# The first step of seven block products moves into the second plain block, and output rows get six buffers

## The chip, the cores and the metric

The kernel runs on one core of a Trainium2 chip. The metric is the device time of one execution in microseconds (us). The runs of the kernel before took 783.31 to 784.70 us, median 784.04. A core has a matrix engine (TensorE, PE in the profile), a vector engine (VectorE, DVE), a scalar engine (ScalarE, ACT), GpSimd (POOL) and SyncE (SP), which issues most transfers. Each engine works through its own list of instructions in the order of the program; semaphores tie the lists together.

## The reference, cut to what matters

```python
# 1. attention without softmax, RMS norm        -> x [2304, 512]
# 2. eight experts, each token goes to one       -> x [2304, 512]
# 3. the dense layer pair, d_model 512, d_ff 2048:
h = x @ w_in                                              # [2304, 2048]
g = np.maximum(h, 0.0) + np.log1p(np.exp(-np.abs(h)))     # softplus
return g @ w_out                                          # [2304, 512]
```

All inputs are float32. The change touches part 3 alone, the last 380 us of the kernel.

## The kernel before, in words

**Precision.** Every float32 operand of a matmul is held as a high part (a cast on ACT) and a low part (value minus high part, on DVE). A product is then three matmuls: high by high, high by low, low by high.

**Tokens.** Part 3 takes the 2304 tokens as two *plain blocks* of 384 and two *passes* of 768 (`NPAS`).

**Plain blocks** (`mlp_step`, L1039). For each of the 16 slices f of 128 hidden units: 12 matmuls of 384 columns (`mlp1`, L951) fill a PSUM bank `tp_t`; softplus follows in three pieces, each one step later than the one before (`soft_a`, `soft_b`, `soft_c`, L971 to L998); then 9 matmuls of 512 columns (`mlp2`, L1017) add the slice into three output banks `acc_t`. So in step f the PE does `mlp1` of f and `mlp2` of f-2, while ACT and DVE do the cast of f-2, the logarithm of f-1 and the absolute value and exponential of f. `side(s)` (L1594) puts work for the passes behind each step: sums and differences of the input blocks (`x_sum`, L1108), their splits (`x_split`, L1101) and those of the weights (`w_sums`, L1120).

**Passes.** Here the first matrix product is taken in 2 by 2 blocks with seven block products instead of eight (the scheme of Strassen and Winograd). A pass has eight *steps* s of 256 hidden units, so there are 16 steps, s = 0 to 15. `prod(s, n)` (L1140) is product n: 6 matmuls of 384 columns into one of two PSUM accumulators, `strip["a"]` and `strip["b"]`, in the order 1, 2, 6, 5, 7, 3, 4. Between products the accumulators are read out: `keep_a(0..2)` and `c12` are copies on ACT (L1165, L1174), `c11`, `c22` and `c21` additions on DVE (L1168, L1171, L1177). A product that starts or goes on in an accumulator has to wait for the read-out before it. The results are two halves of 768 columns, *a* (c11 and c22) and *b* (c21 and c12).

Each half goes through softplus one step later: `pa` is absolute value and exponential on ACT (L1185, L1186) and adding 1 on DVE (L1187); `pa2` a correction on DVE (L1191) and the logarithm on ACT (L1192); `pb` a maximum-and-add and a subtraction on DVE (L1196, L1197); `pc` the cast on ACT (L1203) and the low part on DVE (L1204). `pc` also queues six *units*; a unit (L1213) is three matmuls of 512 columns into one of six output banks. `strip_step` (L1230) writes the order out by hand: products, units and these pieces.

For the first eight steps `w_raw(s+1)` loads raw weights (L1118), `w_sums` makes four sums (L1127), casts them (L1129), takes the low part (L1131) and stores both for the second pass (L1133); `w_load` (L1115) brings the plain weights, `w2_load` (L1138) those of the second layer. All of these stand in SP's list in program order.

**The end of the blocks** (L1630 to L1663). Step 0 has a form of its own: its products 1 and 2 stand between the last two `mlp_step` calls, the other five and half *a* of its softplus behind them.

**Output rows.** `store_rows` (L1006) copies an output bank to a row buffer and sends it off with an indirect transfer of POOL. Odd rows alternate between two buffers `orow`, even rows all use one place in the tile `ma`.

Of the kernel before, what the change touches and what calls it, by code (L numbers as in the profile page):

```python
# [25 lines left out]
def attention_moe_mlp(tc, q, k, v, g_norm, emb, tau, w1, w2, w_in, w_out, out, caps=CAPS):  # L26
# [20 lines left out]
    NBLK = 2  # L47
    blocks = [(i * HB, HB) for i in range(NBLK)]
# [1020 lines left out]
    def plan():  # L1069
# [4 lines left out]
            [xw[:, 1024 * i:1024 * i + 1024] for i in range(4)],  # L1074
# [5 lines left out]
        strip["g"] = [(mr[:, 0:2 * HB], mr[:, 2 * HB:4 * HB]), tuple(t_[:, 0:2 * HB] for t_ in wm[0, 7])]  # L1080
        strip["s"] = [ma[:, 2432 + HB * i:2432 + HB * (i + 1)] for i in range(3)]
# [7 lines left out]
    def x_src(ps, nm, c):  # L1089
# [50 lines left out]
    def prod(s, n):  # L1140

        a, b = strip["a"], strip["b"]
        wop, xop, dst, start = {
            1: ("A11", "B11", a, True), 2: ("A12", "B21", b, True), 6: ("S2", "T2", a, False), 5: ("S1", "T1", a, False),
            7: ("S3", "T3", b, True), 3: ("S4", "B22", a, False), 4: ("A22", "T4", b, False),
        }[n]
        for c in range(2):
            if wop[0] == "A":
                at = (2 * (int(wop[2]) - 1) + c) * 256 + 128 * (int(wop[1]) - 1)
                w = strip["w"][s % 2][0:2]  # L1150
            else:
# [42 lines left out]
    def pb(kind, s):  # L1194
        h, e, u = soft[kind, s]
        nc.vector.scalar_tensor_tensor(out=u, in0=h, scalar=0.0, in1=u, op0=ALU.max, op1=ALU.add)  # L1196
        nc.vector.tensor_tensor(out=u, in0=u, in1=e, op=ALU.subtract)  # L1197

    def pc(kind, s):
        h, e, u = soft[kind, s]  # L1200
        gh, gl = strip["g"][strip["m"] % 2]
        strip["m"] += 1
        nc.scalar.copy(gh, u)  # L1203
        nc.vector.tensor_tensor(out=gl, in0=u, in1=gh.bitcast(F32), op=ALU.subtract)  # L1204
        for i in range(2):
# [24 lines left out]
    def strip_step(s, extra):  # L1230

        todo = [x for x in extra]

        def more(n=1):
# [38 lines left out]
        if s:  # L1273
            pb("b", s - 1)
        more(2)
        c12(s)
        unit(1)
# [313 lines left out]
    pools["ma"] = ma_pool.tile([128, 3584], F32, name="ma")  # L1591
    pools["mr"] = ma_pool.tile([128, 1536], F32R, name="mr")

    def side(s):  # L1594

        if s in (3, 14):
            for p in range(4 * (s // 14), 4 * (s // 14) + 4):
                for i in range(2):
                    nc.sync.dma_start(out=ws[p, i], in_=wm[0, p][i].bitcast(F32))
                    if p % 4 > 1:  # L1600
                        nc.sync.dma_start(out=ws2[p // 4 * 2 + p % 2, i], in_=wm[1, p][i].bitcast(F32))
        f = s - NF
        if f == 2:
            plan()
            strip["raw"] = dp.tile([128, 1024], F32, name="raws", tag="raw64", bufs=2)
            w_raw(0)
        if f == 4:
            sums = dp.tile([128, 1024], F32, name="sums", tag="raw64", bufs=2)
            strip["gen"] = w_sums(0, sums.rearrange("p (j n) -> p j n", j=4))
        if f in (4, 5, 6):  # L1610
            next(strip["gen"])
            next(strip["gen"])
        if f == 9:
            strip["raw"] = dp.tile([128, 1024], F32, name="raws", tag="raw64", bufs=2)
            w_raw(1)
        for nm, split in {
            7: (("B11", 1),), 8: (("T1", 0),), 9: (("B21", 1),), 10: (("T1", 1), ("T2", 0)),
            11: (("T2", 1), ("T3", 0)), 12: (("T4", 0), ("T3", 1)), 13: (("B22", 1),), 14: (("T4", 1),),
        }.get(f, ()):
            for c in range(2):  # L1620
                (x_split if split else x_sum)(0, nm, c)

# [7 lines left out]
    strip["e"] = dp.tile([128, 1024], F32, name="ce", tag="raw64", bufs=2)[:, 0:2 * HB]  # L1630
    strip["a"], strip["b"] = (acc_tile()[:, 0:HB] for _ in range(2))
    x_sums = x2[:, :, 2 * HB:2 * HB + 256]
    w_load(1, (0, 1))
    gen_ = w_sums(1, x_sums)
    prod(0, 1)
    keep_a(0)
    mlp_step(last)
    prod(0, 2)
    mlp_step(last + 1)
    w2_load(2)  # L1640
    w2_load(3)
    while rest:
        store_rows(*rest.pop(0))
    prod(0, 6)
    c11(0)
    keep_a(1)
    prod(0, 5)
    keep_a(2)
    for _ in range(3):
        next(gen_)  # L1650
    prod(0, 7)
    c22(0)
    pa("a", 0)
    pa2("a", 0)
    prod(0, 3)
    c12(0)
    pb("a", 0)
    for _ in range(3):
        next(gen_)
    prod(0, 4)  # L1660
    c21(0)
# [154 lines left out]
```

## Time and profile before

| | us |
|---|---|
| median of the three runs | 784.04 |
| the profiled execution | 786.2 |
| its span, first to last instruction | 784.2 |
| PE busy (92% of the span) | 720.3 |
| DVE busy (72%) | 565.2 |
| ACT busy (56%) | 438.9 |

The profiled execution is 2.0 us longer than its span. Busy time is a union over overlapping instructions, so a PE that runs at the lower of its two clock levels (the profile gives the granted clock as a share of 2.4 GHz, 0.5 being 1.2 GHz) is busy and slow at once. The interesting figure of a stretch is its length against the matmul columns in it. In the profiled execution the second plain block ends near 472 us; step 1 begins at 476.61, step 2 at 501.74, step 3 at 521.02, step 7 at 589.65, step 9 at 627.42, step 11 at 670.19, step 15 at 737.00 us.

### The profile page before, as it was taken

The numbers are of one execution on the slowest core, as the hardware profiler recorded it, in microseconds if no ns is written. First come the engines' busy times: TensorE is split into PE (matmuls) and PEld (weight loads), VectorE is DVE, ScalarE is ACT, GpSimd is POOL, SyncE is SP. The second block draws the span as 40 slices with busy tenths as digits, with TensorE's granted clock in tenths as the row PEclk, the third lists the DMA queues.
The fourth block names the chain that finished last, engine by engine and source line by source line (L and its number), as shares of the span: only waits on it lengthen the run. The fifth ranks groups of instructions, "written<-read, shape, count | busy, mean of one in ns | idle before, by whom it ended". The sixth has DMA issues, their size and how long they took to land.

```text
span 784.2 us, 11874 instructions
## 1 busy us (share of the span) xinstructions
PE 720.3 (92%) x4267; PEld 638.7 (81%) x4267; DVE 565.2 (72%) x990; ACT 438.9 (56%) x783; POOL 265.6 (34%) x203
## 2 busy tenths in 40 slices
PE   8885899999999999999999996899998969999983
PEld 5884599999999999989899885788886858888862
DVE  5589888887887888779767873576777835666661
ACT  2686585575676666567565643455555654454452
POOL 5365168867777876737210001000000030000002
PEclk9997899999999999999999997799999979999998
DMA  9994699988889998563912036433552264245102
GB/s 241 274 291 165 212 299 318 306 265 272 296 272 314 295 310 286 196 232 124 374 41 81 1 108 207 155 134 135 211 218 108 108 241 162 107 134 221 76 0 83
DMA packets 82754, 154.36 MB, mean 197 GB/s; under 512 B 14708, under 2 KB 43404, under 8 KB 82690
## 3 DMA queue, kind: packets, MB, share of 16 engines
q1 hardware_dynamic: 79170, 143.70, 55.7%
q0 software_dynamic: 3344, 9.80, 3.3%
q8 instruction: 35, 0.57, 0.3%
q14 instruction: 29, 0.24, 0.1%
q10 hardware_dynamic: 176, 0.05, 0.0%
HBM read 114.71 MB, written 38.81 MB: 196 GB/s over the span
## 4 chain that ended last, share of the span: by engine, by line
PE 55%; issue 19%; DVE 14%; ACT 7%; DMA 3%; POOL 1%; SPq 1%; ACTq 0%; DVEq 0%; POOLq 0%
PE acc_t L895 9%; PE acc_t L897 8%; PE acc_t L896 8%; PE acc_t L1028 3%; PE acc_t L1027 3%; PE acc_t L1026 3%; PE tp_t L897 3%; PE tp_t L895 3%; PE tp_t L896 3%; PE acc_t L1226 2%; PE tp_t L1332 1%; PE acc_t L1224 1%; PE acc_t L1225 1%; DVE ma L1196 1%; DVE ma L1197 1%
## 5 line engine op out<-in xcount | busy, mean ns | idle before, releaser
L903 POOL TENSOR_TENSOR wl<-st,wh 128x1024 fp32r<-128x1024 f32 x64 | 156.1, 2443 | 57.4 <-ACT wh L901 56.5
L1015 POOL DMA_INDIRECT out_dram<-ma,idx x9 | 8.9, 986 | 317.0 <-ACT ma L1014 315.2
L901 ACT CAST wh<-st 128x1024 fp32r<-128x1024 f32 x72 | 74.7, 1045 | 37.9 <-PE acc_t L896 17.2
L895 PE MATMUL acc_t<-hh,wh 128*128 128x368 f32 (+7 forms) x256 | 81.1, 317 | 0.0
L895 PE MATMUL acc_t<-xh,wh 128*128 128x368 f32 (+7 forms) x256 | 78.5, 307 | 1.1 <-ACT x L1555 0.7
L897 PE MATMUL acc_t<-hh,wl 128*128 128x368 f32 (+7 forms) x256 | 78.1, 305 | 0.9 <-DVE wl L903 0.9
L896 PE MATMUL acc_t<-xl,wh 128*128 128x368 f32 (+7 forms) x256 | 78.2, 305 | 0.0
L896 PE MATMUL acc_t<-hl,wh 128*128 128x368 f32 (+7 forms) x256 | 78.0, 305 | 0.0
L897 PE MATMUL acc_t<-xh,wl 128*128 128x368 f32 (+7 forms) x256 | 78.0, 305 | 0.0
L1192 ACT ACTIVATE ma<-ma 128x768 f32<-128x768 f32 x32 | 27.1, 846 | 63.8 <-DVE ce L1191 63.8
L895 PEld LDWEIGHTS acc_t<-xh,wh 128*128 128x128 f32 x256 | 48.2, 188 | 2.1 <-ACT x L1555 1.4
L1196 DVE SCALAR_TENSOR_TENSOR ma<-x,ma 128x768 f32<-128x768 f32 x32 | 30.7, 958 | 26.3 <-ACT ma L1192 26.3
L895 PEld LDWEIGHTS acc_t<-hh,wh 128*128 128x128 f32 x256 | 48.1, 188 | 1.4 <-DVE hl L1538 0.3
L897 PEld LDWEIGHTS acc_t<-hh,wl 128*128 128x128 f32 x256 | 48.2, 188 | 1.2 <-DVE wl L903 1.2
L896 PEld LDWEIGHTS acc_t<-xl,wh 128*128 128x128 f32 x256 | 48.2, 188 | 0.6 <-DVE xl L1361 0.6
L897 PEld LDWEIGHTS acc_t<-xh,wl 128*128 128x128 f32 x256 | 48.2, 188 | 0.0
L896 PEld LDWEIGHTS acc_t<-hl,wh 128*128 128x128 f32 x256 | 48.2, 188 | 0.0
L1533 ACT ACTIVATE hh<-acc_t 128x368 fp32r<-128x368 f32 (+7 forms) x64 | 27.7, 433 | 23.1 <-PE acc_t L897 22.6
L1187 DVE TENSOR_SCALAR ma<-ce 128x768 f32<-128x768 f32 x32 | 17.9, 559 | 30.9 <-ACT ce L1186 30.8
L1165 ACT COPY ma<-tp_t 128x384 f32<-128x384 f32 x45 | 21.4, 476 | 27.0 <-PE tp_t L1159 26.8
L978 ACT ACTIVATE ma<-tp_t 128x384 f32<-128x384 f32 x30 | 14.8, 492 | 36.0 <-PE tp_t L897 36.0
L1538 DVE SCALAR_TENSOR_TENSOR hl<-acc_t,hh 128x368 fp32r<-128x368 f32 (+7 forms) x64 | 29.9, 474 | 6.6 <-ACT hh L1533 6.4
(410 smaller groups left out, 2201.1 us busy)
## 6 DMA issues: line engine op xcount, KB each, us to landing
st<-in_moe_w_dram SPq DMA_DIRECT2D x64, 512.0 KB
xs<-ws SPq DMA_DIRECT2D x24, 512.0 KB
raw<-in_moe_w_in_dram SPq DMA_DIRECT2D x16, 512.0 KB
raw<-in_moe_w_out_dram SPq DMA_DIRECT2D x16, 512.0 KB
wd<-pre_p SPq DMA_DIRECT2D x32, 256.0 KB
wh<-ws SPq DMA_DIRECT2D x11, 512.0 KB
wl<-ws SPq DMA_DIRECT2D x11, 512.0 KB
ws<-wh SPq DMA_DIRECT2D x10, 512.0 KB
```

Source lines behind the costliest of these rows:

```text
L895: nc.tensor.matmul(ps_, wh, xh, start=start, stop=False)
L896: nc.tensor.matmul(ps_, wh, xl, start=False, stop=False)
L897: nc.tensor.matmul(ps_, wl, xh, start=False, stop=stop)
L901: nc.scalar.copy(h, raw)
L903: eng.tensor_tensor(out=l, in0=raw, in1=h.bitcast(F32), op=ALU.subtract)
L1026: nc.tensor.matmul(mt[b][t_], gh[:, cs_], wh[:, f % 2, :], start=f == 0, stop=False)
L1027: nc.tensor.matmul(mt[b][t_], gh[:, cs_], wl[:, f % 2, :], start=False, stop=False)
L1028: nc.tensor.matmul(mt[b][t_], gl[:, cs_], wh[:, f % 2, :], start=False, stop=f == NF - 1)
L1192: nc.scalar.activation(out=u, in_=u, func=AF.Ln)
L1196: nc.vector.scalar_tensor_tensor(out=u, in0=h, scalar=0.0, in1=u, op0=ALU.max, op1=ALU.add)
L1533: nc.scalar.activation(out=hh[:, m, :C], in_=p[:, :C], func=AF.Relu)
L1538: nc.vector.scalar_tensor_tensor(out=hl[:, m, :C], in0=p[:, :C], scalar=0.0, in1=hh[:, m, :C].bitcast(F32), op0=ALU.max, op1=ALU.subtract)
```

## The change

Three things are done, and buffers are laid out anew to make room for them.

1. **Step 0 stands inside the second plain block.** `side` is given an own table: behind plain step f = 9 come product 1 and `keep_a(0)`, behind 10 product 2, behind 11 product 6, behind 12 product 5, behind 13 product 7 and `c22`, behind 14 product 3, `c12` and the beginning of softplus of half a. Product 4 stands ahead of the call that ends slice 14, the rest of softplus of half a between the calls for slices 14 and 15. Input sums and weight sums start earlier, and weight sums of steps 0 and 1 both end within the block.
2. **Six row buffers for the passes.** Rows 0 and 1 use the two `orow` buffers, rows 2 to 5 free columns of the four parts of `x2`.
3. **Another order in `strip_step`.** The absolute value of half a stands in front of `keep_a(0)`, that of half b in front of `keep_a(2)`; `pc` of half a comes in front of product 5; both DVE pieces of `pb` for b stand together; the four weight sums come in one piece after `keep_a(0)`; step 15 starts softplus of its half a itself. `w_sums` now works in place, in the tile that the raw weights are loaded into.

```diff
     def store_rows(b, t_):
...
-        o = dp.tile([128, DM], F32, name="orow", tag="dec_a", bufs=2) if i % 2 else pools["ma"][:, 5 * HB:5 * HB + DM]
+        if b >= NBLK and t_ > 1:
+            o = x2[:, t_ - 2, 2 * HB:2 * HB + DM]
+        elif i % 2 or b >= NBLK:
+            o = dp.tile([128, DM], F32, name="orow", tag="dec_a", bufs=2)
+        else:
+            o = pools["ma"][:, 5 * BLK:5 * BLK + DM]
...
+    def w_sums(s, raw):
+        a = raw.rearrange("p (k n) -> p k n", k=4)
+        a11, a12, a21, a22 = (a[:, 2 * j:2 * j + 2, 128 * i:128 * i + 128] for i in range(2) for j in range(2))
+        h, l = strip["w"][s % 2][2:4]
+        for o, p, m, op in ((a22, a21, a22, ALU.add), (a21, a11, a21, ALU.subtract), (a11, a22, a11, ALU.subtract), (a12, a12, a11, ALU.subtract)):
+            nc.vector.tensor_tensor(out=o, in0=p, in1=m, op=op)
+            yield
+        nc.scalar.copy(h, raw)
...
     def strip_step(s, extra):
...
         prod(s, 1)
         if ("b", s - 2) in soft:
             pc("b", s - 2)
-        more()
+        if ahead:
+            pa("a", s - 1)
         keep_a(0)
+        more(4)
+        if ahead:
+            pa1("a", s - 1)
+        more(1)
         unit(2)
         prod(s, 2)
-        more(2)
-        if s > 1:
-            pa("a", s - 1)
+        if ahead:
+            pa2("a", s - 1)
         unit(1)
         prod(s, 6)
-        if s > 1:
-            pa2("a", s - 1)
         c11(s)
+        if ahead:
+            pb("a", s - 1)
         keep_a(1)
-        if s > 1:
-            pb("a", s - 1)
-        more()
+        if ahead:
+            pb2("a", s - 1)
+            pc("a", s - 1)
+        more(1)
         unit(3)
         prod(s, 5)
-        if s > 1:
-            pc("a", s - 1)
+        pa("b", s - 1)
         keep_a(2)
         more(2)
         unit(2)
         prod(s, 7)
-        if s:
-            pa("b", s - 1)
+        pa1("b", s - 1)
         c22(s)
-        if s:
-            pa2("b", s - 1)
+        pa2("b", s - 1)
+        if final:
+            pa("a", s)
         unit(2)
         prod(s, 3)
...
+    def side(s):
...
+        if f == 9:
+            strip["a"], strip["b"] = (acc_tile()[:, 0:HB] for _ in range(2))
+            prod(0, 1)
+            keep_a(0)
...
+        if f == 14:
+            strip["e"] = [raw_tile()[:, 0:2 * HB]]
+            prod(0, 3)
+            c12(0)
+            pa("a", 0, x2[:, 1, 0:2 * HB])
+            pa1("a", 0)
...
     w_load(1, (0, 1))
+    next(strip["sums", 1])
+    prod(0, 4)
+    c21(0)
+    pa2("a", 0)
     mlp_step(last)
+    pb("a", 0)
+    pb2("a", 0)
+    pc("a", 0)
     mlp_step(last + 1)
```

ACT's list at the end of the second plain block, before: L978 and L979 are absolute value and exponential of slice 15, L1165 is `keep_a(0)` of step 0, L996 the casts of slices 14 and 15, L986 the logarithm of slice 15, L1014 the row copies, L1185 the absolute value of step 0's half a.

```order
L978 ACTIVATE ma<-tp_t 128x384
L979 ACTIVATE ma<-ma 128x384
L1165 COPY ma<-acc_t 128x384
L996 CAST mr<-ma 128x384
L986 ACTIVATE ma<-ma 128x384
L996 CAST mr<-ma 128x384
L1014 COPY orow<-acc_t 128x512
L1014 COPY ma<-acc_t 128x512
L1014 COPY orow<-acc_t 128x512
L1165 COPY ma<-acc_t 128x384 x2
L1185 ACTIVATE ce<-x_1100 128x768
```

The same place after the change: L1186, L1190, L1196 and L1212 are absolute value, exponential, logarithm and cast of step 0's half a, the three casts of L996 those of slices 13, 14 and 15.

```order
L1186 ACTIVATE raws<-x_1100 128x768
L1190 ACTIVATE raws<-raws 128x768
L996 CAST mr<-ma 128x384
L986 ACTIVATE ma<-ma 128x384
L978 ACTIVATE ma<-tp_t 128x384
L979 ACTIVATE ma<-ma 128x384
L1196 ACTIVATE x_1100<-x_1100 128x768
L996 CAST mr<-ma 128x384
L986 ACTIVATE ma<-ma 128x384
L1212 CAST wh_b_4772<-x_1100 128x768
L996 CAST mr<-ma 128x384
L1019 COPY orow<-acc_t 128x512
```

Each of the three casts that `mlp2` of slices 13 to 15 needs now has an instruction of step 0's half a in front of it.

ACT's list over one step of the first pass, before: L1203 is the cast of a half, L1165 `keep_a`, L1185, L1186 and L1192 absolute value, exponential and logarithm, L1129 the cast of the weight sums, L1174 `c12`.

```order
L1203 CAST wh_b_4772<-ma 128x768
L1165 COPY ma<-tp_t 128x384
L1185 ACTIVATE ce<-x_1100 128x768
L1186 ACTIVATE ce<-ce 128x768
L1192 ACTIVATE ma<-ma 128x768
L1165 COPY ma<-tp_t 128x384
L1203 CAST mr<-ma 128x768
L1165 COPY ma<-tp_t 128x384
L1129 CAST wh_4154<-x_1100 128x1024
L1185 ACTIVATE ce<-x_1100 128x768
L1186 ACTIVATE ce<-ce 128x768
L1192 ACTIVATE ma<-ma 128x768
```

After, from the same cast on: L1212 is the cast, L1186, L1190 and L1196 the three functions, L1164 `keep_a`, L1133 the cast of the weight sums, L1173 `c12`.

```order
L1212 CAST mr<-ma 128x768
L1186 ACTIVATE raws<-x_1100 128x768
L1164 COPY ma<-tp_t 128x384
L1190 ACTIVATE raws<-raws 128x768
L1133 CAST wh_4154<-raws 128x1024
L1196 ACTIVATE ma<-ma 128x768
L1164 COPY ma<-tp_t 128x384
L1212 CAST wh_b_4772<-ma 128x768
L1186 ACTIVATE raws<-x_1100 128x768
L1164 COPY ma<-tp_t 128x384
L1190 ACTIVATE raws<-raws 128x768
L1196 ACTIVATE ma<-ma 128x768
```

The absolute values passed a `keep_a` each, and the cast of the weight sums went from the second half of the step to the first.

On POOL the order of the rows' transfers is the same; the six rows of a pass now leave from six different places, where they alternated between two.

## Rows read from the trace of the kernel before

**Rows 1.** Windows by stage: length, each engine's busy time (count), PEclk, DMA share, GB/s
```profile
456.61:476.61 20.00, 18.45 (x91) 16.03 (x91) 9.13 (x19) 9.37 (x19) 2.92 (x3) 1.00 0.56 183
476.61:501.74 25.13, 15.61 (x62) 12.89 (x61) 11.82 (x18) 8.63 (x13) 0.00 (x0) 0.80 0.47 173
501.74:521.02 19.28, 19.09 (x78) 16.38 (x79) 13.47 (x20) 9.18 (x13) 0.00 (x0) 0.82 0.40 143
521.02:589.65 68.63, 65.22 (x313) 55.97 (x312) 52.38 (x77) 36.79 (x52) 0.00 (x0) 1.00 0.48 176
589.65:627.42 37.77, 33.37 (x157) 27.81 (x156) 29.16 (x45) 22.26 (x38) 0.00 (x0) 1.00 0.30 112
627.42:670.19 42.77, 36.30 (x158) 30.20 (x156) 21.05 (x28) 20.06 (x31) 7.08 (x6) 0.88 0.51 185
670.19:737.00 66.81, 65.44 (x313) 55.74 (x312) 40.74 (x53) 33.39 (x49) 0.00 (x0) 1.00 0.43 158
737.00:784.20 47.20, 31.85 (x133) 24.41 (x131) 20.42 (x26) 18.44 (x27) 5.83 (x6) 0.90 0.10 35
680.95:686.89 5.94, 5.94 (x32) 5.40 (x30) 4.31 (x6) 1.72 (x4) 0.00 (x0) 1.00 0.01 3
```

**Rows 2.** Timeline of PE, two matmuls behind long waits: start, duration, [wait and releaser]
```profile
483.81 0.80 PE L1224 MATMUL acc_t<-wh,mr 128*128 128x512 f32 x1 [6.00 <-ACT mr L1203]
...
761.21 0.80 PE L1224 MATMUL acc_t<-wh_b,mr 128*128 128x512 f32 x1 [2.08 <-ACT mr L1203]
```

**Rows 3.** Chain that ended last, end of step 2: start, share of the chain, what
```profile
514.27 1.05 ACT xs L1129
515.32 0.75 ACT ce L1185
...
516.10 0.86 ACT ce L1186
...
516.98 0.56 DVE ma L1187
517.54 0.47 DVE x L1171
518.00 0.88 DVE ce L1191
...
518.90 0.86 ACT ma L1192
...
519.78 0.97 DVE ma L1196
...
520.77 0.97 DVE ma L1197
...
521.76 0.84 ACT wh_b L1203
...
522.63 0.97 DVE wl_b L1204
```

**Rows 4.** Timeline of all engines behind the load of raw weights for step 2
```profile
484.69 0.46 SPq L1118 DMA_DIRECT2D raws<-wd  x1
...
490.05 0.42 DVE L1127 TENSOR_TENSOR x<-raws 128x256 f32<-128x256 f32 x1 [4.43 <-DMA raws<-wd]
```

**Rows 5.** Groups by line and shape, second plain block: count, busy us, mean ns
```profile
L987 DVE SCALAR_TENSOR_TENSOR ma<-tp_t,ma 128x384 f32<-128x384 f32 x7 | 3.8, 549 | 0.0
...
L986 ACT ACTIVATE ma<-ma 128x384 f32<-128x384 f32 x6 | 3.1, 522 | 0.6 <-DVE ma L982 0.6
L996 ACT CAST mr<-ma 128x384 fp32r<-128x384 f32 x6 | 3.0, 507 | 0.0
```

**Rows 6.** Timelines of ACT and POOL, output rows of both passes
```profile
638.25 0.58 ACT L1014 COPY ma<-acc_t 128x512 f32<-128x512 f32 x1 [5.20 <-DMA out_dram<-ma,idx]
...
777.26 0.58 ACT L1014 COPY ma<-acc_t 128x512 f32<-128x512 f32 x1 [2.61 <-DMA out_dram<-ma,idx]
...
779.39 0.97 POOL L1015 DMA_INDIRECT out_dram<-orow,idx  x1 [0.30 <-DVEq L1710]
```

More of the change, by code (lines that the diff above doesn't have):

```diff
@@ L46, in attention_moe_mlp @@
     NPAS = NTOK // (2 * HB) - 1
-    NBLK = 2
-    blocks = [(i * HB, HB) for i in range(NBLK)]
+    blocks = [(0, HB), (HB, HB)]
+    NBLK = len(blocks)
     assert NTOK == (NPAS + 1) * 2 * HB
@@ L1200, in pc @@
         h, e, u = soft[kind, s]
-        gh, gl = strip["g"][strip["m"] % 2]
+        slot = strip["m"] % 2
+        gh, gl = strip["g"][slot]
         strip["m"] += 1
+        assert all(x[-1] != slot for x in units), (kind, s)
         nc.scalar.copy(gh, u)
@@ L1230, in strip_step, with more @@
     def strip_step(s, extra):
-        todo = [x for x in extra]
-        def more(n=1):
+        todo = list(extra)
+        ahead = s > 1
+        final = s == NS - 1
+        def more(n):
             for _ in range(n):
@@ L1597, in side @@
             for p in range(4 * (s // 14), 4 * (s // 14) + 4):
[L1598 to L1601, printed above, removed]
+                keep_w(p)
         f = s - NF
-        if f == 2:
+        if f == 1:
             plan()
[L1605 to L1615, printed above, removed]
+            for p in range(2):
+                strip["raw"] = raw_tile()
+                w_raw(p)
+                strip["sums", p] = w_sums(p, strip["raw"])
         for nm, split in {
-            7: (("B11", 1),), 8: (("T1", 0),), 9: (("B21", 1),), 10: (("T1", 1), ("T2", 0)),
-            11: (("T2", 1), ("T3", 0)), 12: (("T4", 0), ("T3", 1)), 13: (("B22", 1),), 14: (("T4", 1),),
+            1: (("T1", 0),), 2: (("T3", 0),), 3: (("T2", 0),), 6: (("T1", 1),), 7: (("T2", 1),), 8: (("B11", 1),),
+            9: (("B21", 1), ("T4", 0)), 10: (("T3", 1),), 12: (("B22", 1),), 14: (("T4", 1),),
         }.get(f, ()):
@@ L1621, in side @@
                 (x_split if split else x_sum)(0, nm, c)
+        for p, n in {3: (0, 1), 4: (0, 2), 5: (0, 3), 10: (1, 1), 11: (1, 2), 13: (1, 2)}.items():
+            if p == f:
+                for _ in range(n[1]):
+                    next(strip["sums", n[0]])
+        if f == 9:
+            strip["a"], strip["b"] = (acc_tile()[:, 0:HB] for _ in range(2))
+            prod(0, 1)
+            keep_a(0)
+        if f == 10:
+            prod(0, 2)
+            c11(0)
+        if f == 11:
+            prod(0, 6)
+            keep_a(1)
+        if f == 12:
+            prod(0, 5)
+            keep_a(2)
+        if f == 13:
+            prod(0, 7)
+            c22(0)
+        if f == 14:
[4 more added lines that the diff above has]
+            pa1("a", 0)
     for s in range(2, last):
@@ L1629, in attention_moe_mlp @@
             nc.vector.scalar_tensor_tensor(out=idx2, in0=idx2, scalar=keep, in1=own, op0=ALU.mult, op1=ALU.add)
-    strip["e"] = dp.tile([128, 1024], F32, name="ce", tag="raw64", bufs=2)[:, 0:2 * HB]
-    strip["a"], strip["b"] = (acc_tile()[:, 0:HB] for _ in range(2))
-    x_sums = x2[:, :, 2 * HB:2 * HB + 256]
     w_load(1, (0, 1))
-    gen_ = w_sums(1, x_sums)
-    prod(0, 1)
-    keep_a(0)
+    next(strip["sums", 1])
+    prod(0, 4)
+    c21(0)
+    pa2("a", 0)
     mlp_step(last)
-    prod(0, 2)
+    pb("a", 0)
+    pb2("a", 0)
+    pc("a", 0)
     mlp_step(last + 1)
+    while rest:
+        store_rows(*rest.pop(0))
     w2_load(2)
     w2_load(3)
[L1642 to L1661, printed above, removed]
-    pc("a", 0)
     strip["a"], strip["b"] = (tp_tile()[:, 0:HB] for _ in range(2))
+    strip["s"] = [pools["ma"][:, at:at + HB] for at in (4 * HB, 5 * HB, 5 * BLK)]
     def again(nm, c):
```

90 lines of the change are left out of this document (47 added, 43 removed).

## The prediction

> **What bounds the kernel now.** I read the windows by stage first [rows 1]. How long would a stage be if the PE never waited? In the last row it runs 18 matmuls of 384 columns and 12 of 512, 13,056 columns, in 5.94 us: 0.455 ns per column. A step of seven products and twelve units has 34,560 columns: 15.7 us. A product is 1.05, a unit 0.70, `mlp1` and `mlp2` of a slice 2.1 each. Against that, steps 3 to 6 take 68.63 instead of 62.8, steps 7 and 8 37.77 instead of 31.4, steps 9 and 10 42.77 instead of 31.4, steps 11 to 14 66.81 instead of 62.8. From 456.61 to step 3 there are 45.1 us of columns in 64.41, and step 15 and the tail (28.3) take 47.20. So the PE sets the pace, and some 52 us of it are lost in waits and at the lower clock.
>
> Second, who ends these waits. The matmuls behind the longest ones [rows 2] name the cast of a softplus half. The chain that ended last [rows 3] goes, in every step, through absolute value (0.85), exponential (0.86), plus one (0.56), `c22` (0.47), correction (0.88 to 0.97), logarithm (0.86), two DVE operations (0.97 each), cast (0.84), low part (0.97), and in front of it stands the cast of weight sums (1.05). Third, the output rows: the ACT copy of a row waited 5.20 us for an earlier row's transfer, and 2.61 at the end [rows 6]. ACT is in order, so `keep_a(1)` of step 9 stood behind it, and product 5 behind that.
>
> **The change part by part.** Times count from a place in the program; between engines I add 0.03 (ACT and DVE, from the starts in [rows 3]) or 0.2 (PE to a reader, my choice). The matmuls are the same in number and shape; only order, waits and copies count.
>
> *Slices 9 to 13.* Each now has a product more, 5.2 us of PE time per slice. DVE has five operations of about 0.55 [rows 5] (2.6 us) and at most four more of that size: 4.8, under 5.2. The five products cost their columns, 5.25, and no wait (a wait of up to 1 us in all is possible).
>
> *From slice 14's `mlp1` to step 1 (time 0 where `mlp1` of 14 ends).* Columns: five groups of 2.1 and two products, 12.6. Three casts come late.
> - Cast 13 stands behind `c12`, absolute value and exponential of half a. Product 3 ends at 3.15; lag 0.2, copy 0.47, 0.85, 0.86 and the cast 0.51 [rows 5] give 6.05, `mlp2` of 13 was due at 5.25. With 0.2 for its low part: 1.0 lost.
> - Product 4 ends at 9.4. `c21` needs it (lag and 0.55: 10.1), then the correction 0.97, the logarithm 0.86 and only then cast 14, 0.51: 12.4. `mlp2` of 14 waits 3.0, and 0.1 for the low part.
> - From 12.4: logarithm 15 (0.52) and two operations of 0.55, then two of 0.97 and the cast of half a (0.84), and behind it cast 15 (0.51): 17.1. The PE was free at 14.6 and waits 2.6; the low part stands behind that of half a: 0.6.
>
> Sum 12.6 + 1.0 + 3.1 + 3.2 = 19.9.
>
> *Step 1 (time 0 at product 1).* Half a's units are ready. The raw weights for step 2 are not: their load follows on SP the load that waits for `mlp2` of 15, so it is issued near 1.2. Before, such a load was used 490.05 - 484.69 = 5.4 us after its issue [rows 4], behind 1 MB of stores; here 1 MB of weights is ahead and three rows beside it. I take 6.3 (5.4 to 8): 7.5. The sums now stand early: four (0.42 each) to 9.15, cast 1.05, `keep_a(1)` to 10.65, and product 5, due at 7.35, waits 3.3. `c22` then comes at 13.6 and holds product 4 for 0.5; `c12` stands behind the logarithm and holds product 1 of step 2 for 1.05. Columns 11.55 (six units only) + 4.85 = 16.4. Half b's cast begins 1.6 after step 2 starts, its low part is ready at 3.4 where 1.5 is needed: step 2 has 15.7 + 1.9 + 0.5 = 18.1.
>
> *Clock.* Granted clocks of 0.80 and 0.82 before [rows 1] mean some 10.0 and 6.9 us at 1.2 GHz. Waits of 2.1 us already brought slow matmuls (0.80) [rows 2], so 3.0 and 2.6 us will too. I take 7 us of matmul time at the lower level: 3.5 us (0 to 10).
>
> Product 1 to step 3: 5.25 + 19.9 + 16.4 + 18.1 + 3.5 = 63.15 for 64.41: 1.3 gained (8 gained to 6 lost). The wait of 6.00 is removed, others take its place.
>
> *Steps 3 to 6.* The absolute value of b no longer stands behind `keep_a(2)` and the cast of sums. What is late next is `c22`, which needs product 7: 10.85 + 0.2 after the step's start, then 4.2 as between 517.54 and 521.76 [rows 3]: the cast of b begins at 15.25, 0.45 before the next step. Before, it began 0.74 after (521.76 against 521.02) and the units waited 1.1. Half a is tighter: from the cast of b, 0.84, 0.97, sums 1.6, 0.56, 0.97, 0.86, 0.97, 0.97, 0.84, 0.97 and lags are 9.7, so its low part is there at 9.25, needed at 8.85: 0.4 lost. 16.2, and 16.4 for steps 4 to 6 with two more differences on DVE: 65.4, 3.2 gained (0 to 5).
>
> *Steps 7 and 8.* Eight casts and low parts of inputs replace sums, two casts of them behind `c12`; I get 16.6 and 18.6, as the differences at the end of step 7 hold half b's low part until 2.7 us into step 8. 35.2: 2.6 gained (0 to 5).
>
> *Steps 9 and 10.* Six copies of 0.59 on ACT without a wait, three ahead of `keep_a(1)`, three ahead of b's absolute value, which moves `c22` 0.9 back: 16.1 and 16.6. 32.7: 10.1 gained (7 to 11).
>
> *Steps 11 to 14.* Without sums half a's low part is in time: 15.8 each, 3.6 gained (0 to 4).
>
> *Step 15 and the tail.* At 15.75 eighteen units are left. b of 14 waits 1.1. `c21` ends at 17.6; behind it stand corrections, logarithms, DVE pairs and casts of both halves of step 15, one after another: 0.97, 0.86, 0.97, 0.97, 0.56, 0.97, 0.97, 0.86, 0.97, 0.97, 0.84 less overlaps: the last cast ends at 27.9, the PE was free at 27.0. The first row's copy ends at 29.9; six transfers of POOL follow at 1.27 (0.97 and 0.30 [rows 6]), the last until 37.5; from there 784.20 - 780.36 = 3.84 remain. 41.4 for 47.20: 5.8 gained (3 to 7).
>
> Sum 1.3 + 3.2 + 2.6 + 10.1 + 3.6 + 5.8 = 26.6. The span of 784.2 becomes 757.6, with 2.0 around it 759.6. The median of the runs lies 2.2 under the profiled execution: **757.4 us**.
>
> **The rivals.**
> 1. *Forecast.* Rows, step order and tail gain, the block's end hardly.
> 2. *The block's end gains too.* The raw load is there within 5.4 us, and the clock stays up through the waits. For it: a wait of 5.4 included 1 MB of stores. Against: [rows 2]. Then product 5 waits 2.2 instead of 3.3 and the clock costs nothing: 4.6 less, 753.
> 3. *Only the rows gain.* The sums now live in the raw tile until the low part is taken, so the load of the next raw weights could become the wait in each of steps 2 to 6, and half a could take b's place as the late one. For it: DVE did wait 4.43 once [rows 4]. Against: before, too, the load stood behind the stores of the same sums on SP. Steps 3 to 8, 11 to 14 and step 2 give nothing then: 757.4 + 9.4 + 2 = 769.
> 4. *Slower: the PE falls to 1.2 GHz and stays there.* Place: slice 14 to step 2, where bursts of 2 us stand between waits of 1 to 3. Its columns are 12.6 + 11.55 + 15.7 = 39.9 us; all at half speed, less the 12 us of waits and 3.5 already counted that the slow matmuls fill: +24, 782; held into steps 3 and 4 as well, +31 more. It decides from 27 us of matmul time at the lower level beyond my 7 and the filled waits; then 786 to 810, say 790. For it: the clock before was low twice within 45 us. Against: it came back to 1.00 in steps 3 to 6 [rows 1], which lost 1.1 per step without falling. The Trainium skill, "TensorE: Matmul & The Clock Gate", section "HAM oscillation — how this bites in real kernels", says that short bursts between waits can bring the lower clock back again and again; by that rule it is this rival, 790, and the trace agrees with it only behind waits of 2 us and more.
>
> That the change doesn't do what it says is excluded: the two lists of instructions show product 1 behind slice 9 and six row places.
>
> **How the numbers follow.** Chances: forecast 0.60 (752 to 763), second 0.15, third 0.20, fourth 0.05. The range for 8 in 10 takes the second and most of the third: 749 to 768. A measurement of this kernel tells 0.2% (1.6 us) from no change. Only the fourth is slower, of it 0.04; within 0.2% about 0.01 (a low clock that just eats the gain); faster 0.95.
>
> **What will show it.** In the profile after: `mlp2` of slices 14 and 15 wait some 3 us each for casts; in step 1 DVE waits for `raws` and product 5 for `keep_a`; steps 3 to 6 take 16.2 to 16.4, 11 to 14 15.8; no copy of a row waits for a transfer, and step 9 shows no wait of 4 us; POOL's last six transfers stand 1.27 apart. I am wrong if steps 3 to 6 still take 17, if step 9 takes over 18, if the tail is not under 43, or if the stretch from slice 14 to step 3 differs from 57.9 by over 6.

## The result, and the profile after

The changed kernel took 760.44 to 761.78 us in four runs, median 761.13, against 784.37 for the kernel before: a ratio of 0.9701 (95% interval 0.968 to 0.9722). The prediction was 757.4 (749 to 768). The profiled execution took 761.78, its span is 759.7.

The windows by stage of the kernel after answer to [rows 1] (length, busy time of PE, PEld, DVE, ACT and POOL with counts, granted clock, DMA share, GB/s). They run from the end of slice 14's `mlp1` to step 1, then step 1, step 2, steps 3 to 6, 7 and 8, 9 and 10, 11 to 14, step 15 and the tail.

```profile
464.21:484.08 19.87, 15.39 (x61) 11.43 (x60) 12.60 (x21) 9.63 (x18) 0.32 (x1) 0.91 0.48 159
484.08:503.04 18.96, 14.22 (x62) 12.75 (x60) 5.77 (x10) 5.76 (x10) 2.60 (x3) 0.82 0.74 263
503.04:521.40 18.36, 16.67 (x79) 13.96 (x79) 14.70 (x21) 9.46 (x14) 0.00 (x0) 1.00 0.40 144
521.40:587.19 65.79, 64.76 (x313) 55.72 (x312) 53.45 (x79) 36.57 (x53) 0.00 (x0) 1.00 0.51 184
587.19:622.81 35.62, 32.94 (x157) 27.88 (x156) 27.82 (x43) 21.66 (x39) 0.00 (x0) 1.00 0.32 119
622.81:654.96 32.15, 31.89 (x157) 28.08 (x156) 20.28 (x27) 19.07 (x31) 7.61 (x6) 1.00 0.65 245
654.96:718.37 63.41, 63.41 (x313) 56.11 (x312) 40.75 (x53) 33.06 (x49) 0.00 (x0) 1.00 0.46 166
718.37:759.70 41.33, 30.04 (x133) 23.54 (x131) 20.06 (x26) 18.30 (x27) 5.84 (x6) 0.93 0.11 40
```

Against [rows 1], steps 3 to 6 gained 2.8 us, 7 and 8 2.2, 9 and 10 10.6, 11 to 14 3.4, step 15 and the tail 5.9. At the end of the blocks little came back, and the granted clock is still 0.91 and 0.82 there. The timeline of PE shows the waits that are left (in brackets: the wait and its releaser).

```profile
476.51 0.50 PE L1031 MATMUL acc_t<-wh_b,mr 128*128 128x512 f32 x1 [2.79 <-ACT mr L996]
481.31 0.51 PE L1031 MATMUL acc_t<-wh_b,mr 128*128 128x512 f32 x1 [0.87 <-ACT mr L996]
496.07 0.69 PE L1156 MATMUL tp_t<-wh,xs 128*128 128x384 f32 x1 [4.49 <-ACT ma L1164]
...
547.22 0.50 PE L1235 MATMUL acc_t<-wh_b,wl_b 128*128 128x512 f32 x1 [0.26 <-DVE wl_b L1213]
...
607.44 0.50 PE L1235 MATMUL acc_t<-wh_b,mr 128*128 128x512 f32 x1 [1.89 <-DVE mr L1213]
```

The first two are `mlp2` of slices 14 and 15 waiting for their casts, the third is product 5 of step 1 behind `keep_a(1)`. Each of steps 3 to 8 has one wait of the fourth kind, for half a's low part; the last is half b's low part early in step 8. What held the first: DVE worked through `c21` (L1176) and the correction (L1195), and ACT's cast stood behind the logarithm that needs the correction.

```profile
473.76 0.56 DVE L1176 TENSOR_TENSOR x<-acc_t,x 128x384 f32<-128x384 f32 x1
474.24 0.95 DVE L1195 SCALAR_TENSOR_TENSOR raws<-x,raws 128x768 f32<-128x768 f32 x1
...
475.22 0.84 ACT L1196 ACTIVATE x<-x 128x768 f32<-128x768 f32 x1 [3.82 <-DVE raws L1195]
475.97 0.49 ACT L996 CAST mr<-ma 128x384 fp32r<-128x384 f32 x1
```

And the third: the raw weights for step 2 were issued at 485.12 and first used 7.64 us later; the cast of the sums and `keep_a(1)` follow, so product 5 starts at 496.07 instead of 491.4.

```profile
485.12 0.42 SPq L1123 DMA_DIRECT2D raws<-wd  x1
...
492.76 1.80 DVE L1131 TENSOR_TENSOR raws<-raws 128x256 f32<-128x256 f32 x4 [10.46 <-DMA raws<-wd]
...
494.60 1.04 ACT L1133 CAST wh<-raws 128x1024 fp32r<-128x1024 f32 x1 [8.72 <-DVE raws L1131]
495.55 0.47 ACT L1164 COPY ma<-tp_t 128x384 f32<-128x384 f32 x1
```

Of the rows [rows 6], no copy in the passes waits for a transfer any more, and POOL's last transfers stand 1.28 apart:

```profile
749.42 1.95 ACT L1019 COPY x<-acc_t 128x512 f32<-128x512 f32 x3
...
754.01 0.97 POOL L1020 DMA_INDIRECT out_dram<-x,idx  x1 [0.30 <-issue]
755.29 0.97 POOL L1020 DMA_INDIRECT out_dram<-x,idx  x1 [0.30 <-issue]
```

### The profile page after: what moved, and what is told of

It reads as the page before. It is cut to its first block, busy times and chain, and to the rows that moved or that the text cites. A ratio compares the mean times of both kernels' runs of the same rounds, so it can differ in the third digit from the quotient of the medians.

```text
span 759.7 us, 11868 instructions
## 1 busy us (share of the span) xinstructions
PE 710.8 (94%) x4267; PEld 635.2 (84%) x4267; DVE 562.8 (74%) x990; ACT 436.4 (57%) x783; POOL 265.8 (35%) x203
## 5 line engine op out<-in xcount | busy, mean ns | idle before, releaser
L1020 POOL DMA_INDIRECT out_dram<-orow,idx x7 | 8.2, 1173 | 327.0 <-ACT orow L1019 325.8
L1196 ACT ACTIVATE ma<-ma 128x768 f32<-128x768 f32 x31 | 26.2, 846 | 58.2 <-DVE raws L1195 58.2
L1191 DVE TENSOR_SCALAR ma<-raws 128x768 f32<-128x768 f32 x31 | 17.3, 558 | 20.7 <-ACT raws L1190 20.4
L1235 PE MATMUL acc_t<-wh_b,mr 128*128 128x512 f32 x72 | 29.6, 411 | 2.4 <-DVE mr L1213 2.4
L978 ACT ACTIVATE ma<-tp_t 128x384 f32<-128x384 f32 x30 | 14.7, 491 | 29.0 <-PE tp_t L897 29.0
```

The source lines that it names most:

```text
L1020: nc.gpsimd.indirect_dma_start(out=rows_out[i], out_offset=bass.IndirectOffsetOnAxis(ap=idx2[:, i:i + 1], axis=0), in_=o, in_offset=None)
L1191: nc.vector.tensor_scalar(out=u, in0=e, scalar1=1.0, scalar2=None, op0=ALU.add)
L1196: nc.scalar.activation(out=u, in_=u, func=AF.Ln)
L1235: nc.tensor.matmul(mt[b][t_], gl, wh, start=False, stop=last_)
```

## The experiments

Times are medians of five or six runs unless a stage of a profiled execution is named; the ratios in brackets are to the kernel before, run anew beside each group (medians 783.87 to 785.03). "Up to step 3" is counted from the first `mlp1` of the second plain block, which leaves out what earlier stages vary by (in the profiles of fourteen kernels, with the same code up to there, it began between 393.87 and 397.60 us): 125.37 before, 124.31 after. The medians hold that variation too, so what an edit gives is read more safely from the stages.

**1. Raw weights for step 2 early.**

```diff
     next(strip["sums", 1])
+    w_raw(2)
     prod(0, 4)
...
-            w_raw(s + 1)
+            if s > 1:
+                w_raw(s + 1)
```

> The changed kernel, but the raw weights for step 2 are loaded right after the weight sums of step 1 (issue near 474 us) instead of behind the two loads that wait for the last slice (485.12). After the change they were used 7.64 us after their issue, product 5 of step 1 waited 4.49, and the 20 matmuls behind that wait ran at the low clock. Theory A (the late load alone makes product 5 wait, and the wait brings the low clock): the sums stand before c11, product 5 waits under 0.5, no slow matmuls in step 1; 4.7 of wait and 2.4 of clock go: 754 us. Theory B (the clock falls because of the waits of 2.8 and 0.9 ahead of step 1, not because of this one): product 5 does not wait but products 5 and 7 stay slow: 757. Theory C (the load only changes places with the loads it passes, and another wait of 4 us comes, for second-layer weights or for the weights of step 2): 760 to 762.

Measured: 753.99 (ratio to before 0.9614, 0.9593 to 0.9635). Product 5 no longer waits, and step 1 runs at the full clock:

```profile
483.62:496.72 13.10, 11.99 (x62) 10.54 (x60) 3.97 (x6) 5.67 (x9) 1.95 (x2) 1.00 0.91 340
```

18.96 became 13.10, in spite of the waits ahead of it at slices 14 and 15 (2.79 and 1.43 in this run): the slow matmuls of step 1 belonged to its own wait. Theory A. From the end of slice 14's `mlp1` to step 1 it took 1.0 longer (20.90, clock 0.84), so up to step 3 the gain is 4.9; the median fell by 7.1, but slice 0 also began 1.5 earlier in this profile.

**2. Softplus of half a later: `c21`, correction and logarithm behind the cast of slice 14, the rest behind that of slice 15.**

```diff
     prod(0, 4)
+    mlp_step(last)
     c21(0)
     pa2("a", 0)
-    mlp_step(last)
+    mlp_step(last + 1)
     pb("a", 0)
     pb2("a", 0)
     pc("a", 0)
-    mlp_step(last + 1)
```

> The changed kernel, but c21 and what follows of softplus of half a of step 0 stand behind the casts of slices 14 and 15 on ACT and DVE. Theory A (mlp2 of slices 14 and 15 wait because these casts stand behind the logarithm and the cast of half a): waits of 2.79, 0.87 and 0.31 go, the nine matmuls of mlp2 of slice 14 run at full clock (1.5 us); the low part of half a comes up to 1 us late for the first units of step 1. Sum 4.3 + 1.5 - 0.8 = 5.0 less: 756 us. Product 5 of step 1 still waits 4 to 5 us for the raw load, since that is issued earlier by as much. Theory B (half a is what bounds the block's end, wherever its operations stand): the units of step 1 wait some 4 us instead: 760 to 762.

Measured: 756.0 (0.9643, 0.9622 to 0.9665). The wait at slice 14 went, that at slice 15 grew to 1.78, because the edit, unlike what its expectation says, leaves the logarithm of half a ahead of that cast, and the logarithm needs the correction, which stands behind `c21` on DVE:

```profile
475.64 0.84 ACT L1196 ACTIVATE x<-x 128x768 f32<-128x768 f32 x1 [3.47 <-DVE raws L1195]
476.39 0.49 ACT L996 CAST mr<-ma 128x384 fp32r<-128x384 f32 x1
```

Half a's units wait only 0.26, so Theory B falls. Product 5 waits 3.47; the load took 7.2 us here. So the 5.1 gained fit theory A's 5.0 with other terms than it named.

**3. Both.** The two diffs above together.

> Both edits: raw weights for step 2 early, and half a of step 0 behind the casts of slices 14 and 15. Theory A (two separate losses): the gains add, 7.1 + 5.0 = 12.1: 749 us, and the granted clock is 1.00 from the end of the blocks to the tail. Theory B (a common cause, the load of DVE and ACT at the end of the block, or one clock drop that either edit mends): hardly more than the larger of the two alone, 753 to 755.

Measured: 751.67 (0.9572, 0.955 to 0.9595), 9.5 less than the changed kernel, where the single gains add to 12.3. It lies between the two theories. Up to step 3 it takes 116.18, the singles 119.45 and 118.95: 8.1 gained, where the singles add to 10.2. The clock is still 0.96 and 0.94 around step 1, behind the wait of 1.79 for the cast of slice 15, which neither edit mends.

**4. Two row buffers instead of six.**

```diff
-        if b >= NBLK and t_ > 1:
-            o = x2[:, t_ - 2, 2 * HB:2 * HB + DM]
-        elif i % 2 or b >= NBLK:
+        if i % 2 or b >= NBLK:
```

> The changed kernel with part 2 taken back: all output rows of the passes use the two orow buffers, so the copy of a row waits for the transfer of the row two before it. Theory A (rows were what steps 9 and 10 and half of the tail lost): steps 9 and 10 take 40 to 43 us instead of 32.15, the tail 2 to 3 more: 771 to 774 us. Theory B (the new order, in which keep_a and the absolute values stand elsewhere among the copies, is what gained there): steps 9 and 10 take under 35, 761 to 765.

Measured: 769.44 (0.9811, 0.9789 to 0.9832). Steps 9 and 10, and the tail from step 15 on, with a copy of a row and the product behind it:

```profile
619.88:660.21 40.33, 34.84 (x158) 30.14 (x156) 20.29 (x27) 19.18 (x31) 7.24 (x6) 0.92 0.53 196
723.66:768.50 44.84, 30.04 (x133) 23.56 (x131) 20.06 (x26) 18.29 (x27) 5.81 (x6) 0.91 0.10 37
```

```profile
631.35 0.58 ACT L1017 COPY orow<-acc_t 128x512 f32<-128x512 f32 x1 [6.52 <-DMA out_dram<-orow,idx]
632.37 0.69 PE L1154 MATMUL tp_t<-wh,xs 128*128 128x384 f32 x1 [4.88 <-ACT ma L1162]
```

The rows are worth 8.2 us in steps 9 and 10 and 3.5 in the tail: the mechanism of theory A, 1.6 us below its range. The 8.2 holds some slow matmuls (clock 0.92). The two stages lose 11.7 and the median only 8.3, since slice 0 began 3.0 earlier in this profile.

**5. The order of a step as before, for steps 1 to 14.** The run holds that order in a branch of its own; the diff shows in effect what moves with the absolute values and the weight sums. The cast of half a is behind product 5 again and the input splits of step 7 stand as before.

```diff
-        if ahead:
-            pa("a", s - 1)
         keep_a(0)
-        more(4)
-        if ahead:
-            pa1("a", s - 1)
-        more(1)
...
+        more(2)
+        if ahead:
+            pa("a", s - 1)
+            pa1("a", s - 1)
...
-        pa("b", s - 1)
         keep_a(2)
```

> The changed kernel with the order of a step taken back to that of before for steps 1 to 14 (absolute values behind keep_a, weight sums spread over the step, the cast of half a behind product 5, input splits of step 7 as before). Theory A (the order gives the forecast's terms of steps 3 to 8 and 11 to 14): steps 3 to 6 take 68 to 69 us instead of 65.79, 7 and 8 37.5 to 38 instead of 35.62, 11 to 14 66.5 to 67 instead of 63.41; 9 and 10 about 1 more; sum 8.5 to 10: 770 us. Theory B (a part of it comes from the sums being made in place and other buffers, which stay): 3 to 6 less than that, 765 us.

Measured: 770.59 (0.9825, 0.9803 to 0.9847). Steps 3 to 6 and 11 to 14 are back to [rows 1] within 0.03:

```profile
516.68:585.29 68.61, 65.57 (x314) 55.80 (x313) 52.70 (x77) 36.80 (x52) 0.00 (x0) 1.00 0.48 176
...
658.63:725.47 66.84, 65.48 (x314) 55.74 (x313) 40.75 (x53) 33.41 (x49) 0.00 (x0) 1.00 0.43 158
```

Steps 7 and 8 take 37.67, 9 and 10 35.67. So the order alone gives these terms; that the sums are made in place gives nothing there. In step 1, though, the order of before is the better one:

```profile
482.70:498.75 16.05, 12.21 (x61) 10.45 (x59) 5.57 (x10) 5.88 (x9) 1.94 (x2) 1.00 0.83 306
```

16.05 instead of 18.96: `keep_a(1)` does not stand behind the cast of the weight sums, and PE waits 1.31, 1.73 and 0.79 in place of 4.49 and 0.25, at the full clock. The load was used 6.93 after its issue here.

**6 and 8. Only the absolute value of half b behind `keep_a(2)`, and only that of half a behind `keep_a(0)`.**

```diff
-        pa("b", s - 1)
         keep_a(2)
         more(2)
+        pa("b", s - 1)
```

```diff
-        if ahead:
-            pa("a", s - 1)
         keep_a(0)
+        if ahead:
+            pa("a", s - 1)
```

> The changed kernel, only the absolute value of half b stands behind keep_a(2) again. Theory A (worked out from the rows after: keep_a(2) ends near 9.05 of a step, absolute value, exponential and plus one then near 11.35, where c22 is ready at 11.05; so 0.3 later, which the 0.45 ahead of the next step covers): no change, 760.6 to 761.8. Theory B (as the forecast put it for steps 3 to 6: b's absolute value behind keep_a(2) was what made its cast late): 0.5 to 1 us more per step from 2 to 14, 766 to 772.

> The changed kernel, only the absolute value of half a stands behind keep_a(0) again. Theory A (half a is the tight one: exponential 0.85 later, plus one behind the weight sums 0.45 later; its low part was 0.4 late in steps 3 to 6, and had some 0.5 to spare in steps 11 to 14): 0.45 more in each of steps 2 to 8, 0.3 in each of 9 to 14, sum 3 to 5: 764 to 766. Theory B (the weight sums on DVE hide it, and b sets the pace): no change, 760.6 to 761.8.

Measured: 762.08 (0.9719, 0.9696 to 0.9742) for half b, the same as the changed kernel within the intervals, and 767.5 (0.9793, 0.9765 to 0.9821) for half a. Steps 3 to 6 and 11 to 14 of the kernel with b behind:

```profile
519.87:585.64 65.77, 64.73 (x313) 55.81 (x312) 53.54 (x79) 37.48 (x53) 0.00 (x0) 1.00 0.49 184
654.19:718.18 63.99, 63.99 (x314) 56.25 (x312) 40.39 (x53) 32.83 (x49) 0.00 (x0) 1.00 0.45 165
```

and of the one with a behind:

```profile
522.55:589.39 66.84, 65.66 (x313) 55.78 (x312) 53.78 (x79) 36.32 (x53) 0.00 (x0) 1.00 0.49 181
659.20:726.07 66.87, 65.51 (x313) 55.79 (x312) 40.74 (x53) 32.53 (x49) 0.00 (x0) 1.00 0.44 158
```

Steps 3 to 6 do not care for b's place (65.77 against 65.79), steps 11 to 14 lose 0.58 by it; a's costs steps 3 to 6 1.05, and steps 11 to 14 the whole 3.46 that the order had given there: 0.87 per step, not the 0.3 expected. So half a has nothing to spare there. With a behind, each of steps 11 to 14 waits for its low part, which none of them does in the changed kernel:

```profile
685.65 0.51 PE L1235 MATMUL acc_t<-wh_b,wl_b 128*128 128x512 f32 x1 [0.26 <-DVE wl_b L1213]
```

**7. Step 0's products at the end of the blocks.** The blocks `if f == 9` to `if f == 14` of `side` are gone, and behind them:

```diff
+    prod(0, 1)
+    keep_a(0)
     mlp_step(last)
+    prod(0, 2)
     mlp_step(last + 1)
...
+    prod(0, 6)
+    c11(0)
+    keep_a(1)
...
+    prod(0, 4)
+    c21(0)
+    pc("a", 0)
```

> The changed kernel with part 1 taken back in the place of the products: products 1 and 2 of step 0 between the last two calls of the second block, the other five and softplus of half a behind them, as before; input and weight sums stay early. Theory A (the forecast: the end of the blocks gains hardly, because waits for casts and for the raw load replace the wait for half a): 0 to 4 us more, 761 to 765. Theory B (the move of step 0 is worth far more, and the new waits hide it): over 6 us more, 767 or above. Theory C (the move costs): under 760.

Measured: 756.36 (0.9632, 0.9611 to 0.9653), 4.8 us less than the changed kernel, and the intervals don't meet: theory C. The part that gives the change its name costs time as it is laid out here. Step 1 and the wait for half a that the move was to take away, in this kernel:

```profile
478.08:498.15 20.07, 14.28 (x62) 11.92 (x61) 10.44 (x16) 7.68 (x12) 0.00 (x0) 0.83 0.45 177
```

```profile
484.00 0.80 PE L1233 MATMUL acc_t<-wh,wh_b 128*128 128x512 f32 x1 [4.72 <-ACT wh_b L1212]
```

Up to step 3 it takes 120.80: the early weight sums and the rest gain 4.6 against before, and the move then gives 3.5 of it back.

**9. The whole end of the block laid out anew.** Beside these lines all four weight sums of step 0 stand behind slice 4, the fourth one slice earlier and the first one later than in the changed kernel; their cast and low part stay behind slice 5. Sums, cast and low part of step 1 are all done by slice 13, and the step loop loads the raw weights from step 3 on, as in run 1:

```diff
             pa("a", 0, x2[:, 1, 0:2 * HB])
-            pa1("a", 0)
...
+    w_raw(2)
     w_load(1, (0, 1))
-    next(strip["sums", 1])
+    pa1("a", 0)
     prod(0, 4)
-    c21(0)
-    pa2("a", 0)
     mlp_step(last)
+    h, e, u = soft["a", 0]
+    nc.vector.scalar_tensor_tensor(out=e, in0=u, scalar=-1.0, in1=e, op0=ALU.add, op1=ALU.subtract)
+    g15 = soft_c(sb.pop(last - 1))
+    nc.scalar.activation(out=u, in_=u, func=AF.Ln)
     pb("a", 0)
     pb2("a", 0)
     pc("a", 0)
-    mlp_step(last + 1)
+    c21(0)
+    mlp2(steps[last - 1][0], [(steps[last - 1][1], g15)])
```

> The changed kernel with the whole end of the second block laid out by what the runs before showed: raw weights for step 2 early; exponential of step 0's half a behind the cast of slice 13, its logarithm, subtraction and cast behind the cast of slice 15, but ahead of c21 (which only half b needs); weight sums of step 0 finished one slice later, those of step 1 one slice earlier. Theory A (each named wait is a loss of its own: 0.5 at slice 13, 1.8 at slice 15, 0.9 at slice 5 and 0.3 at slice 3 are left in the run with both edits, 751.7): 3 to 4 less than that, 747.5 to 749. Theory B (half a of step 0 now comes late for the units of step 1): 750 to 753.

Measured: 746.74 (0.9509, 0.9483 to 0.9534), 0.8 below theory A's range. Up to step 3: 112.17. No `mlp2` waits for a cast; half a's first units wait 0.33 and 0.26. Step 0's products now stand in the block without a wait there. From the start of slice 14's `mlp1` to step 1, and step 1:

```profile
458.01:472.67 14.66, 14.66 (x73) 12.89 (x73) 11.11 (x22) 7.84 (x15) 0.00 (x0) 1.00 0.68 248
472.67:487.70 15.03, 12.84 (x62) 10.39 (x60) 7.74 (x13) 7.39 (x12) 3.02 (x3) 1.00 0.81 297
```

**10. Two weight sums ahead of plus one, two behind the correction; half b of step 0 early in step 1.** Here `k` is "a", in step 1 "b":

```diff
         keep_a(0)
-        more(4)
-        if ahead:
-            pa1("a", s - 1)
-        more(1)
+        more(2)
+        pa1(k, s - 1)
         unit(2)
         prod(s, 2)
-        if ahead:
-            pa2("a", s - 1)
+        pa2(k, s - 1)
+        more(3)
```

> The changed kernel, but in each step two of the four weight sums stand ahead of plus one of half a and two behind its correction, under the logarithm; in step 1 softplus of half b of step 0 takes the place that half a has in later steps. Theory A (half a's low part is the one wait of 0.45 in steps 3 to 8, and the sums on DVE ahead of plus one make it late): steps 3 to 8 lose 0.3 to 0.45 less each, 2 to 2.7; the waits of 0.25, 1.17 and 0.26 at the start of step 2 stay, since the late raw load now holds half b; sum: 758 to 759.5. Theory B (the cast of the sums, now behind the logarithm, makes keep_a(1) and product 5 late by as much): 760.5 to 762.

Measured: 758.46 (0.9656, 0.9629 to 0.9685); its interval overlaps that of the changed kernel a little, the stages are clearer. Steps 2, and 3 to 6:

```profile
502.78:518.89 16.11, 16.10 (x80) 14.01 (x79) 13.08 (x19) 9.05 (x14) 0.00 (x0) 1.00 0.45 164
518.89:583.20 64.31, 64.31 (x314) 56.05 (x313) 53.08 (x79) 36.20 (x53) 0.00 (x0) 1.00 0.51 188
```

0.37 less per step in steps 3 to 6, and the wait of 0.26 is gone in each. Step 2 gained 2.25, which I had not expected: half b is early enough in spite of the late load (product 5 of step 1 waited 4.90 here). Steps 7 and 8 lost 1.0 (36.62, clock 0.95), so the time lies in theory A's range with other terms than it named.

**11. The two input differences of step 7 in step 8.**

```diff
-            extra = [again("B11", c) for c in range(2)] + [lambda: None] * 3 + [again(nm, c) for nm in ("B21", "T2", "T1") for c in range(2)] + [summed("T4", c) for c in range(2)]
+            extra = [again("B11", c) for c in range(2)] + [lambda: None] * 3 + [again(nm, c) for nm in ("B21", "T2", "T1") for c in range(2)]
...
-            extra = [again(nm, c) for nm in ("T3", "B22", "T4") for c in range(2)]
+            extra = [again(nm, c) for nm in ("T3", "B22") for c in range(2)] + [summed("T4", c) for c in range(2)] + [again("T4", c) for c in range(2)]
```

> The changed kernel, but the two input differences at the end of step 7 stand in step 8. Theory A (they stand on DVE ahead of half b's low part, which the units of step 8 waited 1.89 for; each takes 0.55): 1.1 less, 760. Theory B (the four casts and low parts of step 7 ahead of them are what is late): no change, 760.6 to 761.8.

Measured: 759.19 (0.9656, 0.9628 to 0.9685), overlapping as in 10. Steps 7 and 8 take 34.71 instead of 35.62, and the wait of 1.89 is 0.95: theory A by the stage.

**12. The edits of 9, 10 and 11 together.**

> All edits of the three kernels beside it in one. Theory A (the gains add, and with the raw weights early the softplus of half b of step 0 gains another 2 to 2.5 at step 2): 741 to 744, PE at the full clock from slice 0 of the second block to the tail, steps 3 to 8 at 15.9 to 16.1 each. Theory B (the waits hide one another): 746 to 749.

Measured: 742.89 (0.946, 0.9433 to 0.9486), faster than both kernels and in theory A's range. From the start of slice 14's `mlp1` to step 1, step 1, step 2, steps 3 to 6, and 7 and 8:

```profile
458.77:473.46 14.69, 14.69 (x74) 12.90 (x73) 11.14 (x22) 7.84 (x15) 0.00 (x0) 1.00 0.68 247
473.46:486.57 13.11, 12.35 (x61) 10.53 (x60) 9.07 (x14) 7.80 (x13) 3.02 (x3) 1.00 0.86 300
486.57:502.93 16.36, 16.24 (x80) 13.97 (x79) 13.07 (x19) 8.95 (x14) 0.00 (x0) 1.00 0.51 193
502.93:567.28 64.35, 64.35 (x313) 56.07 (x312) 53.11 (x79) 36.22 (x53) 0.00 (x0) 1.00 0.52 188
567.28:604.56 37.28, 34.51 (x158) 29.26 (x157) 28.10 (x43) 22.18 (x39) 0.00 (x0) 0.95 0.31 113
```

Up to step 3: 108.29, 16.0 less than after the change. Only the last row lost, and there theory A, which wanted 15.9 to 16.1 per step, fails: in step 8 PE waits 1.26 for the cast of half a, with two low parts and an input difference ahead of `c11` on DVE, and the clock fell to 0.95.

## Why the prediction was right, point by point

- **The sum.** The time lay in the range, 3.7 us above the point. The span is 2.1 longer than forecast: 1.44 of it stood there before the second plain block began (slice 0 at 397.09 instead of 395.65, in code that was not changed), 1.2 arose in slices 3 and 5, below; the other terms leave 0.5 on the good side. The rest, 1.5, is the step from the profiled execution to the median: 2.2 forecast, 0.65 here. Two figures of the prediction don't come out of its rows, and no term uses them: its stages lose 65.8 us against their columns (11.1 of it behind the last matmul), not 52, and steps 3 to 6 had lost 1.5 per step, not 1.1.
- **Rows.** Steps 9 and 10: 32.15 for 32.7 forecast; tail 41.33 for 41.4. Undoing the rows shows 8.2 and 3.5 of the 10.6 and 5.9 gained, undoing the order 3.5 of the former (together a little more than the whole). The remaining 2.4 of the tail fits the early start of step 15's softplus, which no run isolates.
- **Order.** 65.79, 35.62 and 63.41 for 65.4, 35.2 and 63.2: right in size. In steps 3 to 6 the named cause was half wrong: the absolute value of b behind `keep_a(2)` costs nothing there (run 6). In steps 11 to 14 its place is worth 0.58. Half a's absolute value carries 1.05 of the 2.8; the remaining 1.8 (the cast of the weight sums and half a's cast, moved with it) were not told apart. In steps 11 to 14 I credited "without sums half a's low part is in time" without naming what had made it late; it was half a's absolute value behind `keep_a(0)` (run 8). That the new order makes step 1 longer (run 5) was not seen.
- **The end of the blocks.** From the end of slice 14's `mlp1` to step 3 57.19 for 57.9 forecast, through the very waits named: cast 14 (2.79), cast 15 (0.87 and 0.31), the raw load (4.49). The sizes that were off nearly cancel: the load took 7.64, not 6.3, cast 15 cost 1.2 of wait, not 3.2, and product 1 of step 2 waited 0.25, not 1.05. The mechanism was right; that the sum came out within 0.7 is luck. Up to step 3, removing waits gave 4.9 (run 1), 5.4 (run 2) and 12.1 (run 9). The low clock: behind the waits the nine matmuls of `mlp2` of slice 14 took 3.93 us for 2.1, and the fifteen from 496.07 on 4.97 for 2.6, 4.2 together, for which 3.5 stood in the sum.

```profile
476.51:480.44 3.93, 3.92 (x9) 2.43 (x9) 3.40 (x5) 0.81 (x2) 0.00 (x0) 0.58 0.73 274
496.07:501.04 4.97, 4.96 (x16) 4.97 (x16) 2.12 (x4) 1.92 (x3) 0.00 (x0) 0.50 0.88 315
```

- **What the forecast missed.** "The block's end hardly" gains was right, 1.1 up to step 3, but as a sum of plus 4.6 and minus 3.5: the early weight sums gain, the move of step 0 loses. I had not priced the parts apart.
- **Slices 3 and 5.** Only slices 9 to 13 were counted. Fourth sum, cast and low part of step 0's weights come behind one slice (5), and the low part of slice 4 stood behind them: 0.9. With the sums spread otherwise (run 9) this 0.9 is gone. The 0.3 of slice 3 stays in run 9, which has no weight sum there: on DVE the two input differences behind slice 2, new in that place, stand ahead of the low part of slice 1.
- **Rivals.** The second needed the load within 5.4 us: it took 7.64. The third, that only rows gain, fell with run 5. The fourth, slower by a clock that stays low, did not come: 0.91 and 0.82 at the end of the blocks, 1.00 from step 2 to step 14, although bursts between waits of 1 to 5 us stood there. By the Trainium skill, "TensorE: Matmul & The Clock Gate", section "HAM oscillation — how this bites in real kernels", short bursts between waits can bring the low clock back again and again. The trace agrees in that it came back twice within 20 us; from step 2 to step 14, without such bursts, the granted clock was 1.00.

## What to carry to other kernels

When work moves to an earlier place, list for each engine that runs in order what now stands behind it there: here a cast of 0.5 us kept the matrix engine waiting 2.8 us, because it stood behind a logarithm whose input stood behind an addition for another half. Price the parts of a change apart: undoing one at a time showed that the part in the name cost 4.8 us (3.5 of it up to step 3), and two small edits turned it into a gain (run 3, 4.7 under run 7). In a steady loop, look for the chain that ends in a wait of a quarter of a microsecond in each step; in steps 11 to 14, swapping two rows of the order was worth 0.87 us a step (run 8).

## What the runs showed of the hardware

The lower clock does not follow a wait of the same length each time. Half b's low part makes PE wait 1.89 us in step 8 of the changed kernel and of run 1, with the same instructions around it. Windows from the matmul behind that wait on, of the kernel after and then of run 1:

```profile
607.44:612.00 4.56, 4.56 (x23) 4.11 (x24) 4.12 (x9) 1.94 (x4) 0.00 (x0) 1.00 0.54 220
```

```profile
601.13:606.00 4.87, 4.87 (x17) 4.40 (x18) 4.43 (x9) 1.88 (x3) 0.00 (x0) 0.65 0.50 204
```

In the one the granted clock is 1.00 (the upper of the two levels), in the other 0.65 over the stretch, with matmuls of 384 columns of 0.52 instead of 0.34 us. Nine of the fourteen profiles have this wait (1.89 to 1.91 us); the clock fell behind it in four, those of runs 1, 2, 9 and 10. Steps 7 and 8 took 36.1 in runs 1, 2 and 9, and 35.6 in the changed kernel and in runs 3, 4 and 7, where it did not fall. So a wait of 2 us was here a risk of some 0.5 us more, not a fixed price; comparisons of a single stage have to look at its clock first.
